# Retention and a mixture of adapters in one kernel: batch scores alternating with the next unit's transposes, the last two units interleaved, adapter weights loaded later

## The chip, the cores and the metric

The kernel runs on one core of a Trainium2 chip. The metric is the device time in microseconds, here the median of three runs. Engines are named as the profile names them: PE is TensorE (PEld its weight loads), DVE is VectorE, ACT is ScalarE, POOL is GpSimd, SP is SyncE, which issues most of the transfers.

## What is computed

Two layers, one behind the other. The first is retention: causal scores with a decay per head and without a softmax. The second is a mixture of eight low-rank adapters, two of them chosen per token.

```python
# q, k, v: (8, 8, 576, 64) fp32 = (batch, heads, sequence, head size)
scores = (q @ k.T) / sqrt(64)
gamma  = 1 - 2 ** (-5 - h)                          # one per head
ret    = (scores * gamma ** (i - j) for i >= j, else 0) @ v
x      = ret as (batch * seq, heads * head size)     # (4608, 512)
logits = x @ w_gate                                  # 8 experts
w      = softmax over the two largest logits
out    = x + sum over the two of w_e * (x @ A[e]) @ B[e]   # rank 16
```

The kernel cuts the sequence of 576 into four full chunks of 128 and a half chunk of 64. In a chunk the scores are made directly; what came before the chunk enters through a 64x64 state per head (`P`), which is updated from chunk to chunk. A quad is four batches of one chunk (that is what one set of loads brings); a unit is two batches of a quad with all eight heads. There are 16 units of full chunks (0 to 15), and two units of half chunks (16 and 17), each with four batches.

## The kernel before

Each unit goes through stages with one letter each. The order of instructions on PE, DVE and ACT is the order in which they are written; a dependency fixes it. PSUM has eight tiles of one bank (`pp`), which every stage takes from; the framework assigns them and places the waits.

```python
def mm(*args, **kw):                       # line 81: every PE instruction
    chain("pe", nc.tensor.matmul(*args, **kw))
def vec(fn, **kw):                         # line 84: DVE, but for two memsets
    chain("dve", getattr(nc.vector, fn)(**kw))
def act(fn, **kw):                         # line 87: ACT
    chain("act", getattr(nc.scalar, fn)(**kw))
...
# scale_v(t): GpSimd multiplies v of unit t by the decay, in place, 2 instructions
# stage_T(t): 16 transposes of q, two PSUM tiles (pqT), copies by ACT; then the same for k (pkT)
# stage_Q(t): query times state P into px (two tiles)          [not in the first chunk]
def stage_S(t):                            # scores of a full unit
    for b in range(2):
        ps = [pp.tile([128, HP, C], FP32, tag="pb", name=f"ps{ho}") for ho in range(2)]
        for hp in range(HP):
            for ho in range(2):
                mm(ps[ho][:, hp, :], lhsT=s["kT"][rows(ho), b, hp, :],
                   rhs=s["qT"][rows(ho), b, hp, :], start=(hp == 0), stop=True, ...)
        for ho in range(2):
            r = wk.tile([128, HP, C], FP32, tag=f"rt{ho}", name=f"rt{ho}", bufs=4)
            vec("tensor_tensor", out=r, in0=ps[ho],
                in1=tri..., op=ALU.mult)       # causal mask, out of PSUM
# half unit: scores of both halves in pe (two tiles), evicted with a mask into rh
# stage_U(t): k times v into pu; DVE adds P (pn), GpSimd scales it into the new P
# stage_R(t): scores times v, onto px; DVE multiplies by the decay of the row into xT
# stage_B(t): 16 transposes of xT into po (two tiles): the x of "x + sum"
# stage_Z(t): xT times the adapters' A and the gate (AW), into pz; then on DVE:
#             lg (logits), m8 (largest eight), ns (minus the sum of the two largest)
def stage_W(t):                            # routing weights
    for g in range(2):
        act("activation", out=sg[:, g, :], in_=lg[:, g, :], func=AFT.Sigmoid,
            bias=ns[:, g : g + 1], scale=2.0)
    for g in range(2):
        vec("scalar_tensor_tensor", out=cm[:, g, :], in0=lg[:, g, :],
            scalar=m8[:, g, 1:2], in1=sg[:, g, :], op0=ALU.is_ge, op1=ALU.mult)
    for g in range(2):                     # zc = weight * (x @ A), fp16
        vec("tensor_tensor", out=zc..., in0=pz..., in1=cm..., op=ALU.mult)
# stage_X(t): 2 transposes of zc (pzt), copied by ACT into zT
# stage_Y(t): zT times B onto po; 4 copies by ACT into osb; stores by SyncE
...
scale_v(0)
for t in range(NU):
    if units[t][2] == 0:
        issue(quads.index(units[t][:2]) + 2)     # loads, two quads ahead
    if t + 1 < NU:
        scale_v(t + 1)
    if t == 0:
        spin(12)                                 # keeps PE busy while loads come
        stage_T(0, pause=12)
        stage_T(1)
        stage_S(0)
        stage_S(1)
        for u in range(2):
            stage_Q(u); stage_U(u); stage_R(u)
        for ho in range(2):                      # AW[1] is AW[0], halves swapped
            gp.tensor_copy(out=AW[1][rows(ho)], in_=AW[0][rows(1 - ho)])
        for u in range(2):
            stage_Z(u)
        stage_T(2)
        continue
    if t == 1:
        continue
    done = [0, 1] if t == 2 else [t - 1] if t > 2 else []
    if not is_full(t):
        stage_Q(t)
    stage_S(t)
    for u in done: stage_W(u)
    if t + 1 < NU: stage_T(t + 1)
    for u in done: stage_B(u)
    if is_full(t):
        stage_Q(t)
    stage_U(t)
    stage_R(t)
    for u in done: stage_X(u)
    stage_Z(t)
    for u in done: stage_Y(u)
stage_W(NU - 1); stage_B(NU - 1); stage_X(NU - 1); stage_Y(NU - 1)
```

Loads: q, k and v of a quad are 1 MB each, in runs of 256 bytes. The first quad's are followed by the adapter weights (`load_moe`: four transfers of A in runs of 64 bytes, one of the gate, and B from GpSimd's queue), and these by the second quad's.

Of the kernel before, what the change touches and what calls it, by code (L numbers as in the profile page):

```python
# [10 lines left out]
FP32 = mybir.dt.float32  # L11
# [7 lines left out]
def kernel(  # L19
# [141 lines left out]


    nat = {}

    def issue(n):
        if n >= len(quads):
            return
        c, qd = quads[n]
        first = n == 0
        tl = [  # L170
            iop.tile([128, QUAD, H, Dh], FP32, tag=tag, name=tag) for tag in ("q32", "k32", "v32")
        ]
        if c == NFULL:
            for src, dst in zip((q, k, v), tl):
                for g in range(2):
                    nc.sync.dma_start(
                        out=dst[64 * g : 64 * g + 64, 0:2].rearrange("p s h d -> p (s h) d"),
                        in_=src[
                            QUAD * qd + 2 * g : QUAD * qd + 2 * g + 2, :, C * c : C * c + L, :
                        ].rearrange("s h j d -> j (s h) d"),  # L180
                    )
        def load(n, lo, hi):
            nc.sync.dma_start(  # L183
                out=tl[n][:, lo:hi].rearrange("p b h d -> p (b h) d"),
                in_=(q, k, v)[n][
                    QUAD * qd + lo : QUAD * qd + hi, :, C * c : C * c + C, :
                ].rearrange("b h j d -> j (b h) d"),
            )

        if first:  # L190
            for n in range(3):
                load(n, 0, 4)
                if n == 1:
                    nc.sync.dma_start(out=pack, in_=dr_pack.ap())  # L194
            load_moe()
        elif c < NFULL:
            for n in range(3):
                load(n, 0, 4)
        for sl in range(2):
            nat[(c, qd, sl)] = [x[:, 2 * sl : 2 * sl + 2] for x in tl]  # L200

# [19 lines left out]
                op=ALU.mult,  # L221
            )

    def stage_T(t, pause=0):

        q32, k32, v32 = nat[units[t]]
        s = st.setdefault(t, {})
        for src, nm in ((q32, "qT"), (k32, "kT")):
            if nm == "kT":
                spin(pause)  # L230
            dst = s[nm] = wk.tile([128, 2, HP, C], FP32, tag=nm, name=nm)
            ps = [pp.tile([128, HP, 2, L], FP32, tag="pb", name=f"p{nm}") for _ in range(2)]
            for hp in range(HP):
# [20 lines left out]
    def stage_Q(t):  # L254
        c, qd, sl = units[t]
        s = st[t]
        s["px"] = px = [
            pp.tile([128, HP, C], FP32, tag="pb", name=f"px{x}") for x in range(2)
        ]
        if c == 0:  # L260
            return
        full = is_full(t)
        for hp in range(HP):
            for y in range(1 if full else 2):
                for ho in range(2):
                    for x in range(2):
                        Pt = P[2 * qd + sl][:, :, x] if full else P[2 * qd + x][:, :, y]
                        i = slice(0, C) if full else rows(y)
                        mm(
                            px[x][rows(ho ^ x), hp, i],  # L270
                            lhsT=Pt[rows(ho), hp, :],
                            rhs=s["qT"][rows(ho), x, hp, i],
                            start=(hp == 0 and y == 0),
                            stop=False,
                            skip_group_check=True,
                        )

    def stage_S(t):
        s = st[t]
        rt = s.setdefault("rt", {})  # L280
        if not is_full(t):
# [20 lines left out]
                )  # L302
                rt[ho] = r
            return
        for b in range(2):
            ps = [pp.tile([128, HP, C], FP32, tag="pb", name=f"ps{ho}") for ho in range(2)]
            for hp in range(HP):
                for ho in range(2):
# [102 lines left out]
                    )  # L411
        s["po"] = po

    def stage_X(t):
        s = st[t]
        pzt = pp.tile([128, 2, 128], FP16, tag="pb", name="pzt")
        for g in range(2):
            mm(
                pzt[:, g, :], lhsT=s["zc"][:, g, :], rhs=ident16,
                is_transpose=True, start=True, stop=True,  # L420
            )
        zt = mo.tile([128, 2, 128], FP16, tag="zT", name="zT")
        act("copy", out=zt, in_=pzt)
        s["zT"] = zt

    def stage_Z(t):
        s = st[t]
        pz = pp.tile([128, 2, ER + E], FP32, tag="pb", name="pz")
        for g in range(2):
            for dt in range(HP):  # L430
                mm(
                    pz[:, g, :],
                    lhsT=s["xT"][g][:, dt, :],
                    rhs=AW[g][:, dt, :],
                    start=(dt == 0),
                    stop=(dt == HP - 1),
                    skip_group_check=True,
                )
        m8 = mo.tile([128, 2, E], FP32, tag="m8", name="m8")
        ns = mo.tile([128, 2], FP32, tag="ns", name="ns")  # L440
        sg = mo.tile([128, 2, E], FP32, tag="sg", name="sg")
        cm = mo.tile([128, 2, E], FP32, tag="cm", name="cm")
        lg = mo.tile([128, 2, E], FP32, tag="lg", name="lg")
        vec("tensor_copy", out=lg, in_=pz[:, :, ER : ER + E])
        for g in range(2):
            vec("max", out=m8[:, g, :], in_=lg[:, g, :])
        vec("scalar_tensor_tensor", 
            out=ns, in0=m8[:, :, 0], scalar=-1.0, in1=m8[:, :, 1],
            op0=ALU.mult, op1=ALU.subtract,
        )  # L450
        s["route"] = lg, m8, ns, sg, cm, pz

    def stage_W(t):
        s = st[t]
        lg, m8, ns, sg, cm, pz = s.pop("route")
        for g in range(2):
            act("activation", 
                out=sg[:, g, :], in_=lg[:, g, :], func=AFT.Sigmoid,
                bias=ns[:, g : g + 1], scale=2.0,
            )  # L460
        for g in range(2):
            vec("scalar_tensor_tensor", 
                out=cm[:, g, :], in0=lg[:, g, :], scalar=m8[:, g, 1:2], in1=sg[:, g, :],
                op0=ALU.is_ge, op1=ALU.mult,
            )
        zc = mo.tile([128, 2, ER], FP16, tag="zc", name="zc")
        for g in range(2):
            vec("tensor_tensor", 
                out=zc[:, g, :].rearrange("p (e r) -> p e r", e=E),
                in0=pz[:, g, 0:ER].rearrange("p (e r) -> p e r", e=E),  # L470
                in1=cm[:, g, :].unsqueeze(2).broadcast_to((128, E, R)),
                op=ALU.mult,
            )
        s["zc"] = zc

    def stage_Y(t):
        c, qd, sl = units[t]
        s = st.pop(t)
        po = s["po"]
        osb = outp.tile([128, 2, HP, 2, Dh], FP32, tag="osb", name="osb")  # L480
        bv = Bcat.rearrange("p (a o d) -> p a o d", a=HP, o=2)
        for cc in range(2):
            for g in range(2):
                mm(
                    po[cc][:, g, :, :],
                    lhsT=s["zT"][:, g, :],
                    rhs=bv[:, :, cc ^ g, :],
                    start=False,
                    stop=True,
                    skip_group_check=True,  # L490
                )
        for cc in range(2):
            for g in range(2):
                act("copy", out=osb[:, g, :, cc ^ g, :], in_=po[cc][:, g])
        of = osb.rearrange("p g a o d -> p g (a o d)")
        for g in range(2):
            for x in range(1 if c < NFULL else 2):
                bt = 2 * sl + g if c < NFULL else 2 * g + x
                n0 = S * (QUAD * qd + bt) + C * c
                if c < NFULL:  # L500
                    nc.sync.dma_start(out=out[n0 : n0 + C, :], in_=of[:, g, :])
                else:
                    nc.sync.dma_start(out=out[n0 : n0 + L, :], in_=of[rows(x), g, :])

    issue(0)
    issue(1)
# [14 lines left out]
    for t in range(NU):  # L521
# [3 lines left out]
            scale_v(t + 1)  # L525
        if t == 0:
            spin(12)
            stage_T(0, pause=12)
            stage_T(1)
            stage_S(0)  # L530
            stage_S(1)
            for u in range(2):
# [2 lines left out]
                stage_R(u)  # L535
            for ho in range(2):
                gp.tensor_copy(out=AW[1][rows(ho)], in_=AW[0][rows(1 - ho)])
            for u in range(2):
                stage_Z(u)
            stage_T(2)  # L540
            continue
        if t == 1:
            continue
        done = [0, 1] if t == 2 else [t - 1] if t > 2 else []
        if not is_full(t):
            stage_Q(t)
        stage_S(t)
        for u in done:
            stage_W(u)
        if t + 1 < NU:  # L550
            stage_T(t + 1)
        for u in done:
            stage_B(u)
        if is_full(t):
            stage_Q(t)
        stage_U(t)
        stage_R(t)
        for u in done:
            stage_X(u)
        stage_Z(t)  # L560
        for u in done:
            stage_Y(u)
    stage_W(NU - 1)
    stage_B(NU - 1)
    stage_X(NU - 1)
    stage_Y(NU - 1)
    return

# [28 lines left out]
```

## Time and profile before

| | |
|---|---|
| time, median of three runs | 206.25 us (205.06 to 207.9) |
| the profiled execution | 203.81 us, span of its instructions 202.1 us |
| PE busy | 184.5 us, 91% of the span |
| DVE, ACT, POOL busy | 109.4, 71.5, 58.3 us |
| loads and stores | 28.91 MB read, 9.44 MB written, 190 GB/s over the span |
| TensorE clock granted | 0.99 |

A unit's step is the stretch from its first score matmul to the next unit's. The table shows where some begin, read from the timeline of PE (us from the start of the span).

| event on PE | starts at |
|---|---|
| first transposes of unit 0 | 7.17 |
| scores of unit 0 | 13.12 |
| scores of unit 2 | 29.82 |
| scores of unit 3 | 42.40 |
| scores of unit 4 | 51.62 |
| scores of two later neighbours | 102.62 and 112.83 |
| stage Q of unit 16, the first half unit | 175.23 |
| stage Q of unit 17, the second | 183.97 |
| last product (`po` of unit 17) | 195.33 |

How to read the lines further down: in the page's first part each engine has its busy time, its share of the span and its count of instructions. In the chain, each line has a start, a length and what the time went to. In the timeline, a line has start, length, engine, operation, the tiles written and read, shapes and a count where neighbours were merged; the bracket at its end is the idle time of the engine before it, and what ended that. A tile keeps its name in the code without its number. Each fp32 matmul shows as two instructions, so a full unit's 16 score matmuls are 32. The profile models the ends of matmuls, so that a PE with gaps of a tenth of a microsecond or two can still show as busy.

### The profile page before, as it was taken

The numbers are of one execution on the slowest core, as the hardware profiler recorded it, in microseconds if no ns is written. First come the engines' busy times: TensorE is split into PE (matmuls) and PEld (weight loads), VectorE is DVE, ScalarE is ACT, GpSimd is POOL, SyncE is SP. The second block draws the span as 40 slices with busy tenths as digits, with TensorE's granted clock in tenths as the row PEclk, the third lists the DMA queues.
The fourth block names the chain that finished last, engine by engine and source line by source line (L and its number), as shares of the span: only waits on it lengthen the run. The fifth ranks groups of instructions, "written<-read, shape, count | busy, mean of one in ns | idle before, by whom it ended". The sixth has DMA issues, their size and how long they took to land.

```text
span 202.1 us, 8056 instructions
## 1 busy us (share of the span) xinstructions
PE 184.5 (91%) x3588; PEld 164.6 (81%) x3588; DVE 109.4 (54%) x270; ACT 71.5 (35%) x196; POOL 58.3 (29%) x68
## 2 busy tenths in 40 slices
PE   7889977999999999999999999899999999989740
PEld 2378966899999999999999999799999999978620
DVE  0249628648647565757555655646464646363420
ACT  2040054163525252525243434234343434343060
POOL 5059108043046203636203722610502060200000
PEclk9999999999999999999999999999999999999995
DMA  4996999999999949952989798439145702022044
GB/s 122 312 241 90 296 275 246 284 276 254 322 310 270 289 175 272 274 181 109 250 245 303 247 257 267 111 88 255 51 135 122 194 11 100 3 107 99 11 104 104
DMA packets 47698, 38.73 MB, mean 192 GB/s; under 512 B 18352, under 2 KB 43056, under 8 KB 47664
## 3 DMA queue, kind: packets, MB, share of 16 engines
q1 hardware_dynamic: 47520, 38.09, 66.0%
q8 instruction: 28, 0.46, 1.0%
q0 software_dynamic: 144, 0.13, 0.4%
q14 instruction: 6, 0.05, 0.1%
HBM read 28.91 MB, written 9.44 MB: 190 GB/s over the span
## 4 chain that ended last, share of the span: by engine, by line
PE 79%; DVE 7%; SPq 4%; DMA 3%; ACT 2%; POOL 1%; issue 1%; ACTq 0%; POOLq 0%
PE px L81 22%; PE pz L81 17%; PE ps L81 13%; PE po L81 9%; PE pu L81 9%; PE pkT L81 3%; PE pqT L81 3%; DMA v<-in_v_dram 3%; DVE rt L84 2%; SPq L183 2%; DVE cm L84 2%; SPq L194 2%; PE pzt L81 2%; POOL v L217 1%; ACT osb L87 1%
## 5 line engine op out<-in xcount | busy, mean ns | idle before, releaser
L84 DVE TENSOR_TENSOR rt<-ps,tri 128x512 f32<-128x512 f32 x64 | 39.6, 682 | 13.4 <-PE ps L81 13.4
L217 POOL TENSOR_TENSOR v<-v,pack 128x512 f32<-128x512 f32 x36 | 36.5, 1043 | 23.7 <-DMA v<-in_v_dram 23.7
L349 POOL TENSOR_TENSOR P<-pn,gdec 128x512 f32<-128x512 f32 x12 | 15.3, 1273 | 82.2 <-DVE pn L84 82.2
L81 PE MATMUL pz<-AW,xT 128*128 128x136 f32 x288 | 37.2, 283 | 1.1 <-DVE xT L84 1.1
L81 PEld LDWEIGHTS pz<-AW,xT 128*128 128x128 f32 x288 | 34.5, 190 | 1.6 <-DVE xT L84 1.6
L81 PE MATMUL ps<-qT,kT 64*128 64x128 f32 x512 | 32.6, 278 | 1.6 <-ACT kT L87 1.4
L81 PEld LDWEIGHTS ps<-qT,kT 64*128 64x128 f32 x512 | 29.7, 188 | 4.6 <-PE po L81 2.7
L87 ACT COPY osb<-po 128x256 f32<-128x256 f32 x72 | 21.5, 389 | 30.0 <-PE po L81 28.2
L81 PE MATMUL px<-rt,v 128*64 128x128 f32 x512 | 30.8, 273 | 0.0
L84 DVE TENSOR_TENSOR xT<-px,asc 128x512 f32<-128x512 f32 x36 | 24.7, 691 | 7.3 <-PE px L81 6.0
L87 ACT COPY qT<-pqT 128x512 f32<-128x512 f32 x32 | 17.2, 590 | 31.3 <-PE pqT L81 31.3
L81 PEld LDWEIGHTS px<-rt,v 128*64 128x64 f32 x512 | 27.8, 137 | 0.0
L87 ACT COPY zT<-pzt 128x256 f16<-128x256 f16 x18 | 6.6, 373 | 53.8 <-PE pzt L81 53.8
L87 ACT COPY kT<-pkT 128x512 f32<-128x512 f32 x36 | 19.6, 608 | 9.7 <-PE pkT L81 9.7
L81 PE MATMUL pu<-v,k 128*64 128x64 f32 x512 | 18.6, 225 | 1.4 <-DVE zc L84 1.0
L81 PEld LDWEIGHTS pu<-v,k 128*64 128x64 f32 x512 | 16.4, 138 | 3.9 <-issue 3.1
L84 DVE TENSOR_TENSOR pn<-pu,P 128x512 f32<-128x512 f32 x12 | 8.3, 691 | 20.4 <-PE pu L81 20.4
L81 PE MATMUL po<-id,xT 64*128 64x64 f32 x288 | 15.7, 229 | 2.2 <-DVE zc L84 1.6
L84 DVE COPY lg<-pz 128x16 f32<-128x16 f32 x18 | 3.1, 174 | 25.8 <-PE pz L81 25.8
L81 PEld LDWEIGHTS po<-id,xT 64*128 64x128 f32 x288 | 12.1, 139 | 4.4 <-DVE rt L84 2.4
L81 PE MATMUL px<-qT,P 64*64 64x128 f32 (+1 forms) x512 | 15.6, 262 | 0.0
L81 PEld LDWEIGHTS px<-qT,P 64*64 64x64 f32 x512 | 12.5, 133 | 1.3 <-issue 0.4
(42 smaller groups left out, 147.3 us busy)
## 6 DMA issues: line engine op xcount, KB each, us to landing
out_dram<-osb SPq DMA_DIRECT2D x32, 256.0 KB, 3.3
q<-in_q_dram SPq DMA_DIRECT2D x4, 256.0 KB, 4.4
k<-in_k_dram SPq DMA_DIRECT2D x4, 256.0 KB, 3.7
v<-in_v_dram SPq DMA_DIRECT2D x4, 256.0 KB, 4.0
out_dram<-osb SPq DMA_DIRECT2D x8, 128.0 KB, 2.3
AW<-in_moe_A_dram SPq DMA_DIRECT2D x4, 64.0 KB, 3.5
q<-in_q_dram SPq DMA_DIRECT2D x8, 0.2 KB, 6.3
k<-in_k_dram SPq DMA_DIRECT2D x8, 0.2 KB, 9.1
```

The costliest lines, as they stand in the source:

```text
L81: chain("pe", nc.tensor.matmul(*args, **kw))
L84: chain("dve", getattr(nc.vector, fn)(**kw))
L87: chain("act", getattr(nc.scalar, fn)(**kw))
L183: nc.sync.dma_start(out=tl[n][:, lo:hi].rearrange("p b h d -> p (b h) d"), in_=(q, k, v)[n][QUAD * qd + lo : QUAD * qd + hi, :, C * c : C ...
L194: nc.sync.dma_start(out=pack, in_=dr_pack.ap())
L217: nc.gpsimd.tensor_tensor(out=vv[:, b], in0=vv[:, b], in1=gv[:, 0 if is_full(t) else 1].unsqueeze(2).broadcast_to((128, H, Dh)), op=ALU.mult,)
L349: nc.gpsimd.tensor_tensor(out=Pt, in0=pn, in1=gdec, op=ALU.mult)
```

## The change

1. **Scores and transposes alternate.** In a full unit's step, the scores of the first batch come first, then the q transposes of the next unit, then the scores of the second batch, then the k transposes. The sigmoid (new stage V) is issued on ACT ahead of the q copies. This is to give DVE time to empty the first two score tiles while PE does something else.
2. **The start.** The q transposes of units 0 and 1 come before the k transposes of both. Unit 0's routing and output are done before unit 2 begins, with the transposes of unit 2 between Z(0) and Z(1). Before, units 0 and 1 were both routed in step 2.
3. **The adapter weights** are loaded behind the second quad's q instead of ahead of it.
4. **The last two units** (half chunks) are interleaved; the final one is handled in two halves, so that the routing of one lies beside matmuls of the other, and its output copies are split between ACT and DVE. To have it so, unit 16 holds batches 0, 1, 4 and 5, and unit 17 the others; their loads are one set of six transfers for all eight batches.

```diff
@@ load of quads @@
         if c == NFULL:
+            if qd > 0:
+                return
             for src, dst in zip((q, k, v), tl):
                 for g in range(2):
-                    nc.sync.dma_start(... 2 batches of the quad, 64 rows ...)
+                    nc.sync.dma_start(... 4 batches of one half of the batches, 64 rows ...)
...
-            load_moe()
-        elif c < NFULL:
+        else:
             for n in range(3):
                 load(n, 0, 4)
+                if quads[1] == (c, qd) and n == 0:
+                    load_moe()
@@ stage_T, stage_S: in parts @@
-    def stage_T(t, pause=0):
+    def stage_T(t, names=("qT", "kT")):
...
-    def stage_S(t):
+    def stage_S(t, bs=(0, 1)):
...
-        for b in range(2):
+        for b in bs:
@@ X, Z, W, Y take gs, the halves they work on; V is cut out of W @@
+    def stage_V(t, gs=BOTH):           # the sigmoids
...
+    def stage_Y(t, gs=BOTH, spread=False):
...
+                if spread and cc == 1:
+                    vec("tensor_copy", out=osb[:, g, :, cc ^ g, :], in_=po[cc][:, g])
+                else:
+                    act("copy", out=osb[:, g, :, cc ^ g, :], in_=po[cc][:, g])
@@ the loop @@
             spin(12)
-            stage_T(0, pause=12)
-            stage_T(1)
+            stage_T(0, ("qT",))
+            stage_T(1, ("qT",))
+            spin(10)
+            stage_T(0, ("kT",))
+            stage_T(1, ("kT",))
             stage_S(0)
             stage_S(1)
...
-            for u in range(2):
-                stage_Z(u)
-            stage_T(2)
+            stage_Z(0)
+            stage_W(0)
+            stage_T(2, ("qT",))
+            stage_Z(1)
+            stage_T(2, ("kT",))
+            stage_B(0)
+            stage_X(0)
+            stage_Y(0)
             continue
...
+        if t == NU - 1:
+            break
+        if is_full(t):
+            stage_S(t, (0,))
+            stage_V(t - 1)
+            stage_T(t + 1, ("qT",))
+            stage_S(t, (1,))
+            stage_W(t - 1)
+            stage_T(t + 1, ("kT",))
+            stage_B(t - 1)
             stage_Q(t)
+            stage_U(t)
+            stage_R(t)
+            stage_X(t - 1)
+            stage_Z(t)
+            stage_Y(t - 1)
+            continue
+
+        stage_Q(t)                      # t = 16
         stage_S(t)
+        stage_W(t - 1)
+        stage_T(t + 1)
+        stage_B(t - 1)
         stage_R(t)
+        stage_Q(t + 1)
+        stage_X(t - 1)
         stage_Z(t)
+        stage_W(t)
+        stage_Y(t - 1)
+        stage_S(t + 1)
+        stage_B(t)
+        stage_X(t)
+        stage_R(t + 1)
+        stage_Y(t)
+        for g in range(2):
+            stage_Z(t + 1, (g,))
+            stage_W(t + 1, (g,))
+        stage_B(t + 1)
+        for g in range(2):
+            stage_X(t + 1, (g,))
+            stage_Y(t + 1, (g,), spread=True)
```

## The prediction

> **What bounds the kernel now.** I read the page first, for engine shares and the chain that ended last.
>
> ```profile
> span 202.1 us, 8056 instructions
> ...
> PE 184.5 (91%) x3588; PEld 164.6 (81%) x3588; DVE 109.4 (54%) x270; ACT 71.5 (35%) x196; POOL 58.3 (29%) x68
> ...
> PE 79%; DVE 7%; SPq 4%; DMA 3%; ACT 2%; POOL 1%; issue 1%; ACTq 0%; POOLq 0%
> ```
>
> TensorE is the bound: 79% of the chain. The change takes away no arithmetic (same matmuls, transposes and evictions), so it can only close holes in TensorE's stream. The view by stretches tells where they are (columns: length, then busy time of PE, weight load, DVE, ACT, POOL, clock, DMA share, GB/s).
>
> ```profile
> 0.00:27.00 27.00, 23.88 (x314) 17.82 (x314) 12.29 (x24) 3.60 (x6) 10.86 (x24) 1.00 0.85 214
> 27.00:42.40 15.40, 12.08 (x221) 10.94 (x221) 8.65 (x23) 6.06 (x17) 4.05 (x4) 1.00 0.96 272
> 42.40:123.00 80.60, 80.44 (x1553) 74.30 (x1552) 49.37 (x119) 32.72 (x92) 28.98 (x27) 1.00 0.85 253
> 123.00:134.30 11.30, 10.30 (x201) 9.44 (x200) 7.21 (x17) 4.06 (x12) 5.32 (x5) 1.00 0.53 141
> 134.30:175.20 40.90, 40.78 (x793) 37.55 (x792) 23.15 (x62) 15.98 (x45) 9.11 (x8) 1.00 0.41 112
> 175.20:202.10 26.90, 17.01 (x515) 14.55 (x514) 8.76 (x31) 9.03 (x29) 0.00 (x0) 0.92 0.28 80
> ```
>
> The holes are in unit 2's step (3.3 us idle of 15.4), one step near 123 us (1.0 of 11.3) and the tail of the two half chunks (9.9 of 26.9). The thirteen full steps between (units 3 to 15) look full. I then read the chain in order of time (start, length, what) for the first hole:
>
> ```profile
> 27.72 0.67 ACT qT L87 x2
> 28.39 0.28 issue
> 28.67 1.10 ACT kT L87 x2
> 29.82 1.21 PE ps L81 x16
> 31.03 2.46 DVE rt L84 x4
> 33.49 1.87 DVE cm L84 x2
> 35.36 0.41 DVE zc L84 x2
> 35.82 0.71 PE po L81 x15
> ```
>
> Unit 2's scores wait for its own transposes' copies; then two routings queue behind the four score evictions, and a transpose waits for `zc`. That `cm`, 1.87 us here, is usually 0.35 for two. The timeline of VectorE and GpSimd around the other hole shows the cause:
>
> ```profile
> 125.27 4.05 POOL L217 TENSOR_TENSOR v<-v,pack 128x512 f32<-128x512 f32 x4 [4.33 <-DMA v<-in_v_dram]
> ...
> 126.62 1.72 DVE L84 SCALAR_TENSOR_TENSOR cm<-lg,m,sg 128x8 f32<-128x8 f32 x2
> ...
> 128.88 1.15 PE L81 MATMUL pu<-v,k 128*64 128x64 f32 x32 [0.98 <-DVE zc L84]
> ```
>
> The pair ends at 128.34, just as the third of GpSimd's 1.01 us `v` scalings does (125.27 + 3 x 1.01 = 128.30). Last, inside a "full" step, the weight loads:
>
> ```profile
> 104.40 0.63 PEld L81 LDWEIGHTS pqT<-id,q 64*128 64x128 f32 x16
> 104.95 0.59 PEld L81 LDWEIGHTS pkT<-id,k 64*128 64x128 f32 x16
> 105.45 0.14 PEld L81 LDWEIGHTS po<-id,xT 64*128 64x128 f32 x1
> 105.75 0.57 PEld L81 LDWEIGHTS po<-id,xT 64*128 64x128 f32 x15 [0.16 <-DVE rt L84]
> 106.39 0.86 PEld L81 LDWEIGHTS px<-qT,P 64*64 64x64 f32 x32
> ```
>
> `po` begins at 105.45, takes one transpose and stops until 105.75: it wants a PSUM bank that a score eviction still reads. `po` undisturbed takes 0.64 us in the tail (178.72 to 179.36); here it takes 0.94. So about 0.28 us per step is lost that the busy share hides.
>
> [...] `cm` reads `lg` and `sg`, both in SBUF; the longest took 1.077 us against a median of 0.218. [...] 80.44 busy of 80.60 conceals the 0.28 above. [...] the trace shows the score evictions (0.62 apart) falling behind the scores (0.95 us for two).
>
> **The change, part by part.**
>
> Start. The four transposes of units 0 and 1 are regrouped, but the scores still wait for k and then for ScalarE's copies (13.12), and R(1) still ends near 23.0, paced by `v` (15.57) and GpSimd. No gain there. The adapter loads go behind quad 1's q. Quad loads land about 4.05 us apart (v at 31.3 and 43.3 are three loads apart), so the adapter weights land near 23.3 instead of before 19.6, and their swapped copy (GpSimd, 1.3) near 24.7. Z(0) then runs 23.3 to 24.3, waits, 24.8 to 25.8: a loss of about 0.9. In return W(0)'s VectorE/ScalarE chain lies beside T(2) of q, Z(1), T(2) of k (0.5 + 1.9 + 0.5, to 28.7) and B(0); X(0) waits for the copies of kT ahead of zT on ScalarE (1.1), Y(0) ends near 31.0. S(2) starts then, no longer followed by unit 0's B, X, Y (1.4) or held by two routings. Step 2 takes about 9 instead of 12.6 (29.82 to 42.40), so S(3) starts near 40.0: gain 2.4. But `v` of quad 2 lands at 43.3 as before, DMA being at 0.96; in the earlier step 3 its scaling now meets `cm`, and Z(3) waits some 0.6 to 0.8. Start: **1.7**.
>
> Steady steps. Before, the second bank that `po` takes is that of the third score tile, free at 105.68. With two score tiles, two transposes, two score tiles, two transposes, eight banks being reused in the order they come free, I expect `po` to get the banks of the first two, free by 105.1: the 0.28 goes. Against it two more changes between matmuls and transposes, each 0.05 (scores to transposes, 104.46 to 104.51) to 0.14 (16 transposes take 0.50 before more transposes, 0.64 before matmuls). Net about 0.1 x 13: **1.3**.
>
> Collisions of `cm` with GpSimd. W still follows all four evictions, so the exposure stays; where they fall depends on when `v` lands. I allow **0.3** of the 1.0 us.
>
> Tail, from the start of Q(16), with lengths from the tail before: Q16 to 0.9, S16 2.0, T17 3.1, B15 3.75, R16 5.0, Q17 6.0, X15 6.1, Z16 8.0 (its `xT` was made under Q17; before, it waited 0.73), Y15 8.6, S17 9.65, B16 10.3, X16 10.6. R17 waits for the second `rh` (behind W16's routing on VectorE, 11.7), 12.9; Y16 13.4; Z17 waits for xT, 13.8 to 15.75; B17 16.4 covers the first half's routing; X, zT, Y of half 0 to 17.5, of half 1 to 18.75; two copies in parallel on ScalarE and VectorE 19.35. Two stores instead of four, 0.6 each: 20.6; and the 2.96 us from the last issue (199.14) to the end: 23.6 instead of 26.9. **3.3**.
>
> The half chunk's loads become 6 instead of 12; they have been waited for by nothing on the chain: 0.
>
> Sum: 1.7 + 1.3 + 0.3 + 3.3 = 6.6, and 206.25 − 6.6 = 199.6. The tail is conservatively counted, so I round to 199.3.
>
> **The rivals.** (1) The alternation makes a new PSUM wait: the second score pair then needs a bank of `po` of the unit before, which ScalarE empties in 1.20 us beginning at 102.51. I reckon that free at 103.1 for a tile wanted at 104.1, but the assignment isn't visible. A stall of 0.3 per step would cost 4 us and leave about 204. (2) The later adapter weights cost more than reckoned: they are 64-byte runs, DMA moves only 21 to 106 GB/s between 15.2 and 19.2, and SyncE took 6.37 us to issue them. Sitting in front of k1 they can hold T(2), k1 being due near 27.5. The start would then bring nothing: 201. (3) Nothing in the steady step: 201. (4) The optimistic one: the whole 0.28, no collisions, 2.4 at the start, 4 in the tail: 195.
>
> **Range and chances.** Tail gain is nearly certain (2.5 to 4), start 0 to 3, steps −2 to 3. Together 195.5 to 203. Two per cent is 202.1; missing it needs rival 1, or 2 and 3 together. Faster 0.83, same 0.15, slower 0.02.
>
> **What would show it.** The tail from Q(16) to the end about 23.6; S(3) starting near 40; a step near 10.1 with `po` taking 0.64 between its first weight load and Q's; Z(0) waiting for AW. Wrong, if score matmuls show idle behind `osb` or `rt`, or if `cm` of over 1 us turns up in more steps than three.

## The result and the profile after

| | before | after |
|---|---|---|
| time, median of four runs each | 205.66 us (204.39 to 207.9) | 195.03 us (194.63 to 195.82) |
| ratio, 95% interval | | 0.951 (0.944 to 0.957) |
| span of the profiled execution | 202.1 us | 193.2 us |

The head of the page of the changed kernel:

```profile
span 193.2 us, 8031 instructions
...
PE 180.5 (93%) x3586; PEld 162.5 (84%) x3586; DVE 109.7 (57%) x274; ACT 72.7 (38%) x195; POOL 58.3 (30%) x68
```

The work is the same. PE's count and the other engines' busy times have hardly moved, and only the holes are fewer. PE's busy time fell by 4.0 us, although it does the same matmuls: part of what was closed had been counted as busy.

The view by stretches of the changed kernel, cut where units begin (start to Z(0), to S(2), S(3), S(4), Q(16), end):

```profile
0.00:23.36 23.36, 18.72 (x278) 13.65 (x278) 11.44 (x20) 3.57 (x6) 9.55 (x22) 1.00 0.81 203
23.36:31.44 8.08, 6.96 (x87) 5.98 (x87) 2.25 (x13) 2.91 (x8) 1.32 (x3) 1.00 0.97 278
31.44:40.36 8.92, 8.92 (x168) 8.43 (x167) 5.62 (x14) 4.10 (x12) 3.99 (x4) 1.00 0.92 266
40.36:49.74 9.38, 9.13 (x167) 8.47 (x166) 6.66 (x17) 4.10 (x12) 4.05 (x4) 1.00 0.81 244
49.74:169.72 119.98, 119.77 (x2377) 111.58 (x2377) 73.50 (x182) 49.28 (x133) 39.38 (x36) 1.00 0.72 208
169.72:193.20 23.48, 16.98 (x515) 14.39 (x514) 10.19 (x35) 8.77 (x28) 0.00 (x0) 0.91 0.32 92
```

Unit 2's step is full now (8.92 busy of 8.92). Set beside the same cuts of before, the 8.9 us between the two spans split so:

| stretch | before | after | gain | predicted |
|---|---|---|---|---|
| start of the span to S(4) | 51.62 | 49.74 | 1.88 | 1.7 |
| S(4) to Q(16), twelve steps | 123.61 | 119.98 | 3.63 | 1.3 + 0.3 |
| Q(16) to the end | 26.87 | 23.48 | 3.39 | 3.3 |

Of the first line, 0.52 belongs to the first k, which landed at 10.73 instead of 11.25. What is left, 1.36, is the order of work. The middle line was predicted at less than half its size.

A step before had its `po` stop. The weight loads of the changed kernel in the step that starts at 100.05 (start, length, tiles written and read, count):

```profile
100.93 0.63 PEld L81 LDWEIGHTS pqT<-id,q 64*128 64x128 f32 x16
101.47 0.98 PEld L81 LDWEIGHTS ps<-qT,kT 64*128 64x128 f32 x16
102.37 0.63 PEld L81 LDWEIGHTS pkT<-id,k 64*128 64x128 f32 x16
102.92 0.58 PEld L81 LDWEIGHTS po<-id,xT 64*128 64x128 f32 x16
103.57 0.86 PEld L81 LDWEIGHTS px<-qT,P 64*64 64x64 f32 x32
```

`po` is one line of 16 now, with no wait in it: 102.92 to 103.57 is 0.65 us, where it was 0.94. Eleven of the twelve steps take 9.95 to 9.96; before, the undisturbed ones took 10.19 to 10.26.

The collision, from the timeline of the changed kernel over all engines:

```profile
123.21 4.04 POOL L226 TENSOR_TENSOR v<-v,pack 128x512 f32<-128x512 f32 x4 [5.34 <-DMA v<-in_v_dram]
123.80 1.48 DVE L84 SCALAR_TENSOR_TENSOR cm<-lg,m,sg 128x8 f32<-128x8 f32 x2
124.51 1.15 PE L81 MATMUL pu<-v,k 128*64 128x64 f32 x32
125.20 0.48 DVE L84 TENSOR_TENSOR zc<-pz,cm 128x128 f16<-128x128 f32 x2
```

It is still there: `cm` takes 1.48 under a `v` scaling. But `pu` begins 0.69 before `zc`, so it no longer waits for it. This step, 119.95 to 129.91, took 9.96, like its neighbours; before, such a step took 11.25.

Then the start, where Z(0) and Y(0) wait (PE's timeline):

```profile
23.39 1.17 PE L81 MATMUL pz<-AW,xT 128*128 128x136 f32 x8 [0.49 <-issue]
24.86 1.19 PE L81 MATMUL pz<-AW,xT 128*128 128x136 f32 x8 [0.31 <-POOL AW L570]
...
30.90 0.61 PE L81 MATMUL po<-Bcat,zT 128*128 128x256 f16 x4 [0.79 <-ACT zT L87]
31.44 1.16 PE L81 MATMUL ps<-qT,kT 64*128 64x128 f32 x16
```

And the tail of the changed kernel:

```profile
176.12 2.07 PE L81 MATMUL pz<-AW,xT 128*128 128x136 f32 x16
...
183.23 2.12 PE L81 MATMUL pz<-AW,xT 128*128 128x136 f32 x16 [0.23 <-DVE xT L84]
...
186.96 0.39 PE L81 MATMUL po<-Bcat,zT 128*128 128x256 f16 x2 [0.73 <-ACT zT L87]
...
187.98 0.39 PE L81 MATMUL po<-Bcat,zT 128*128 128x256 f16 x2 [0.36 <-ACT zT L87]
...
188.41 0.42 DVE L84 COPY osb<-po 128x256 f32<-128x256 f32 x1 [0.54 <-PE po L81]
```

Z(16) follows without a wait; before, PE stood idle for 0.56 ahead of it, for `xT`. The last product starts at 187.98, 18.26 after Q(16); before it was 20.10 after (195.33 − 175.23), and its copies then ran for 1.20 more on ScalarE alone. The other 1.55 us of the gain lie behind that product: copies on two engines, and two stores instead of four after the last.

### The profile page after: what moved, and what is told of

Read it like the earlier page. It is cut to its first block, busy times and chain, and to the rows that moved or that the text cites. A ratio compares the mean times of both kernels' runs of the same rounds, so it can differ in the third digit from the quotient of the medians.

```text
span 193.2 us, 8031 instructions
## 1 busy us (share of the span) xinstructions
PE 180.5 (93%) x3586; PEld 162.5 (84%) x3586; DVE 109.7 (57%) x274; ACT 72.7 (38%) x195; POOL 58.3 (30%) x68
## 5 line engine op out<-in xcount | busy, mean ns | idle before, releaser
L84 DVE TENSOR_TENSOR rt<-ps,tri 128x512 f32<-128x512 f32 x64 | 41.0, 686 | 18.7 <-PE ps L81 14.4
L81 PE MATMUL pz<-AW,xT 128*128 128x136 f32 x288 | 37.7, 283 | 1.3 <-issue 0.5
L81 PE MATMUL ps<-qT,kT 64*128 64x128 f32 x512 | 35.7, 281 | 0.7 <-ACT kT L87 0.7
L81 PEld LDWEIGHTS ps<-qT,kT 64*128 64x128 f32 x512 | 31.0, 188 | 3.7 <-PE po L81 2.7
L87 ACT COPY zT<-pzt 128x256 f16<-128x256 f16 (+1 forms) x19 | 6.9, 361 | 48.9 <-PE pzt L81 48.9
L84 DVE COPY lg<-pz 128x16 f32<-128x16 f32 (+1 forms) x19 | 3.3, 173 | 25.8 <-PE pz L81 25.8
L87 ACT ACTIVATE sg<-lg,ns 128x8 f32<-128x8 f32 x36 | 9.4, 318 | 17.6 <-DVE ns L84 17.6
L81 PE MATMUL pqT<-id,q 64*128 64x64 f32 x288 | 11.9, 223 | 1.4 <-DMA q<-in_q_dram 1.4
```

## Experiments

All are variants of the changed kernel with parts put back, or of the kernel before. The half units keep their new grouping of batches and their six loads in every variant of the changed kernel. Each was timed in three rounds or more beside the kernel before on the same chip; a ratio is to those runs. The three parts of the change each gain less than 2% alone, so their intervals are wide beside their gains, and the stretches of the traces tell more.

### One part at a time

**alt_only**: the alternation alone; the start, the place of the adapter weights and the tail as before.

```diff
-            stage_Z(0); stage_W(0); stage_T(2, ("qT",)); stage_Z(1)
-            stage_T(2, ("kT",)); stage_B(0); stage_X(0); stage_Y(0)
+            stage_Z(0); stage_Z(1); stage_T(2)
 ...                                   # adapter weights ahead of the second quad, units 16 and 17 in turn
```

> Only the alternation of scores and transposes (units 2 to 15), with the old start, the old tail and the adapter weights ahead of quad 1. Bank theory (the steady gain is that po no longer waits for the third score eviction and pu no longer for zc): a full step of 9.95 us instead of 10.20, no 1 us loss where cm meets a v scaling, first score of unit 4 to Q of unit 16 in 119.5 to 120.5 us instead of 123.6; in all 3 to 5 us faster than before. Rival (the step got shorter because the new start shifted when v lands, so that collisions fell elsewhere): the step stays at 10.1 to 10.2 and the gain is under 2 us.

Measured: 202.5 us, ratio 0.987 (0.979 to 0.995). S(4) to Q(16) took 119.94, as in the changed kernel, and Q(16) to the end 27.06, as before. So the whole gain of the steps comes from the alternation. One step of the twelve took 10.45, and its lines say why (VectorE, GpSimd, weight loads):

```profile
61.56 2.04 POOL L225 TENSOR_TENSOR v<-v,pack 128x512 f32<-128x512 f32 x2
...
61.91 0.71 DVE L84 SCALAR_TENSOR_TENSOR ns<-m 128x2 f32<-128x2 f32 x1
...
63.69 0.85 PEld L81 LDWEIGHTS ps<-qT,kT 64*128 64x128 f32 x13 [0.20 <-DVE rt L84]
```

Here the `v` scaling met `ns`, normally 0.16, which stands ahead of the score evictions; the second pair of score tiles then lacked a bank. A hold ahead of the evictions still costs. By its ratio the run gained 2.7 us, less than the 3 to 5 expected, while the stretch came out as expected.

**start_only**: the new start and the later adapter weights alone.

```diff
-            stage_S(t, (0,)); stage_V(t - 1); stage_T(t + 1, ("qT",))
-            stage_S(t, (1,)); stage_W(t - 1); stage_T(t + 1, ("kT",))
+            stage_S(t); stage_V(t - 1); stage_W(t - 1); stage_T(t + 1)
 ...                                   # units 16 and 17 in turn
```

> Only the new start (with the adapter weights behind quad 1's q), steps and tail as before. Expected from the two traces: unit 3's scores at 40 to 41 us instead of 42.4, step 10.20, 1 to 3 us faster in all. If the parts are not additive (the start's gain eaten by a later wait for v), under 1 us.

Measured: 202.98 us, ratio 0.988 (0.980 to 0.996). In the profiled execution the first k landed late, at 12.68, so its instants are read from there: S(4) 39.39 us after it, against 40.37 before and 39.01 with the whole change. The steps are 10.20 again, but for one of 11.55 (123.48 to 135.03), where a pair of `cm` was held for 2.02 and `pu` waited 1.28 for `zc`, as it did before.

**tail_only**: the interleaved tail alone.

```diff
 ...                                   # start, adapter weights and full steps as before
         stage_Q(t)                    # t = 16
         stage_S(t)
         stage_W(t - 1); stage_T(t + 1); stage_B(t - 1); stage_R(t)
         stage_Q(t + 1); stage_X(t - 1); stage_Z(t) ...
```

> Only the interleaved last two units. Expected: Q of unit 16 to the end 23.3 to 23.8 us instead of 26.9, 3 to 4 us faster in all. If the tail's gain needed the alternation's bank order, under 2.5 us.

Measured: 202.26 us, ratio 0.986 (0.979 to 0.993). Q(16) to the end took 23.44, against 23.48 with the whole change; the steps 10.20 with one of 11.08. By the ratios the three parts bring 1.3%, 1.2% and 1.4%, each give or take 0.8. Their sum, 3.9%, agrees with the 4.9% of the whole within that. The parts add up as far as these runs can tell, and none visibly gives back what another wins. The tail's time gained 2.9 us by its ratio, where 3 to 4 was expected.

**tail_whole**: the changed kernel, with the last unit's Z, W, X and Y whole instead of by halves.

```diff
-        for g in range(2):
-            stage_Z(t + 1, (g,)); stage_W(t + 1, (g,))
+        stage_Z(t + 1); stage_W(t + 1)
         stage_B(t + 1)
-        for g in range(2):
-            stage_X(t + 1, (g,)); stage_Y(t + 1, (g,), spread=True)
+        stage_X(t + 1); stage_Y(t + 1)
```

> The changed kernel with the interleaved tail, but the last unit routed and written out whole, as before, instead of in two halves with copies on two engines. From the traces: the halves overlap 1.0 to 1.3 us of routing and save about 0.6 us of copies and stores at the end; 0.8 to 2 us slower than the changed kernel. If interleaving the two units is all of the tail's gain: within 0.4 us.

Measured: 197.27 us, ratio 0.959 (0.953 to 0.965); Q(16) to the end 25.53. PE's timeline shows the waits that the halves had covered:

```profile
187.08 0.43 PE L81 MATMUL pzt<-ident,zc 128*128 128x128 f16 x2 [1.14 <-DVE zc L84]
188.03 0.61 PE L81 MATMUL po<-Bcat,zT 128*128 128x256 f16 x4 [0.52 <-ACT zT L87]
```

So of the 3.39 us of the tail 2.05 (25.53 − 23.48) are the halves with the split copies, and 1.34 the interleaving of units 16 and 17.

### The start: adapter weights and loads

**moe_first**: the changed kernel with the adapter weights ahead of the second quad, as before.

```diff
+            load_moe()                # behind the first quad
 ...
-                if quads[1] == (c, qd) and n == 0:
-                    load_moe()
```

> The changed kernel, but with the adapter weights ahead of quad 1 again. By the prediction's reckoning Z of unit 0 then starts at 22.9 to 23.1 instead of 23.39 and its second half does not wait for the swapped copy; but quad 1's q lands near 23.2 and k where it did, so unit 2's k transposes stay bound by the same landing (27.3 to 27.6). Expected: the same within 0.7 us, or up to 0.9 faster. If the placement is what makes the new start work, 1 us slower or more.

Measured: 196.08 us, ratio 0.956 (0.950 to 0.962). S(3) starts 29.4 after the first k's landing, against 29.63 with the weights later. The place of the weights alone is worth nothing that these runs can tell: the median is 1.05 us above the changed kernel's, but the intervals of the two ratios overlap. The instants are a rough comparison, since in this execution the scores of units 0 and 1 took 5.47 us (from 14.17) where the changed kernel's took 3.84, as they would with about 3.3 us at half the clock (an estimate from the two lengths), and the second quad's k was transposed at 29.83, against 28.69.

**split_head**: an attempt at a better start. The first quad's loads are halved, the adapter weights follow at once, units 0 and 1 are finished before unit 2, and GpSimd scales `v` ahead of its other work.

```diff
-            for n in range(3):
-                load(n, 0, 4)
+            for lo in (0, 2):
+                for n in range(3):
+                    load(n, lo, lo + 2)
+            load_moe()
```

> The changed kernel with a start that goes after what is left there: TensorE begins its scores at 12.6 us, because it waits for whole-quad loads. The first quad's loads are cut into halves of two batches, unit by unit, the adapter weights follow directly, GpSimd scales v of unit 0 ahead of its constants, and units 0 and 1 are run one after the other and both finished before unit 2. Expected: scores of unit 0 at 8 to 10 us, of unit 3 at 37 to 39 instead of 40.4; 1.5 to 4 us faster than the changed kernel. If the landing of quad 1's k and v (27 and 31 us) sets the start whatever the first quad does: under 1 us.

Measured: 196.75 us, ratio 0.960 (0.952 to 0.968): no better. Unit 0's scores start at 9.86 instead of 12.60, but S(2) at 32.80 instead of 31.44 and S(3) at 40.76 instead of 40.36. The 1.5 to 4 us expected did not come. PE's timeline says what held unit 2:

```profile
30.14 0.61 PE L81 MATMUL po<-Bcat,zT 128*128 128x256 f16 x4 [1.14 <-ACT zT L87]
30.68 0.71 PE L81 MATMUL pkT<-id,k 64*128 64x64 f32 x16
32.80 1.16 PE L81 MATMUL ps<-qT,kT 64*128 64x128 f32 x16 [1.41 <-ACT kT L87]
...
35.82 1.15 PE L81 MATMUL pu<-v,k 128*64 128x64 f32 x32
```

The second quad's k was issued at 19.20 and landed near 28.3, an estimate from the median of 9.1 that loads of k took in the profile of before. Its transposes stand behind unit 1's output in this order, which waited for ScalarE, and began at 30.68; the scores then waited for ScalarE again. `v` landed near 32.5 (its scaling, which waited for it, began at 32.59), and `pu`, the first to use it, began at 35.82 without a wait. So it was this order, with ScalarE's copies in it, and not the loads, that held unit 2. Whether an order with k's transposes ahead of unit 1's output would gain was not tried. The changed kernel keeps the lowest median of all that ran.

### What the alternation removes, and what it costs

**q_between**: old start and tail, no alternation. Only stage Q moves between the q and the k transposes, so `po` comes 1.0 us later and its bank is long free.

```diff
             stage_S(t)
             stage_W(t - 1)
-            stage_T(t + 1); stage_B(t - 1); stage_Q(t)
+            stage_T(t + 1, ("qT",)); stage_Q(t); stage_T(t + 1, ("kT",)); stage_B(t - 1)
             stage_U(t)
```

> The earlier run with U ahead of B also moved the state's update ahead of Q, so it could not answer. Here, with scores not alternating and the old start and tail, only Q moves: between the q and the k transposes of the next unit, so that po asks for its banks 1.03 us later and the banks it gets are those of the fourth score tile and the first q tile. Bank theory: the 0.3 us stop inside po goes; against it two changes of tile shape more (0.11 us each), so a step of 9.95 to 10.1 instead of 10.20 and 1 to 3.5 us faster than before. Rival (alternating scores with transposes is itself what shortens the step): the step stays at 10.2 to 10.4, time same or slower.

Measured: 203.95 us, ratio 0.988 (0.979 to 0.997). S(4) to Q(16), all of it at a granted clock of 1.00, took 121.65 against 123.61; a step 10.05. The weight loads of one:

```profile
107.65 0.86 PEld L81 LDWEIGHTS px<-qT,P 64*64 64x64 f32 x32
108.69 0.58 PEld L81 LDWEIGHTS pkT<-id,k 64*128 64x128 f32 x16 [0.17 <-issue]
109.18 0.58 PEld L81 LDWEIGHTS po<-id,xT 64*128 64x128 f32 x16
109.83 1.01 PEld L81 LDWEIGHTS pu<-v,k 128*64 128x64 f32 x32
```

`po` takes 0.65 (109.18 to 109.83) without a stop. So the bank was what stopped it (which bank the trace doesn't show), and time alone, without alternation, cures it. It gains 0.15 per step where the alternation gains 0.25: the q transposes, now ahead of Q's 64x64 tiles, take 0.59 (107.07 to 107.66) where they took 0.50. One step, 125.27 to 136.31, still cost about 1 us for `cm`.

**fine_alt**: the changed kernel with scores and transposes alternating twice as often, by groups of 8: four changes more per step.

```diff
+            for b, nm in ((0, "qT"), (1, "kT")):
+                for h2 in ((0, 1), (2, 3)):
+                    stage_S(t, (b,), h2)
+                    stage_T(t + 1, (nm,), h2)      # V and W where they were
```

> The changed kernel with scores and transposes alternating twice as finely: four more changes between matmuls and transposes in each of 14 steps, nothing else. As predicted (0.05 to 0.14 us for a change): 3 to 6 us slower than the changed kernel. If a change between the two costs nothing because both use tiles of 64 rows by 128 columns: within 1 us of the changed kernel, step 9.9 to 10.05.

Measured: 201.33 us, ratio 0.983 (0.975 to 0.991), 6.3 us over the changed kernel, of which the twelve steps are 4.1 (124.08 against 119.98): one takes 10.33, which is 0.38 more than 9.95. Most of that isn't the changes themselves (weight loads):

```profile
106.23 0.54 PEld L81 LDWEIGHTS ps<-qT,kT 64*128 64x128 f32 x8
106.68 0.14 PEld L81 LDWEIGHTS pkT<-id,k 64*128 64x128 f32 x1
106.99 0.26 PEld L81 LDWEIGHTS pkT<-id,k 64*128 64x128 f32 x6 [0.17 <-DVE rt L84]
```

The four groups of scores take 2.04 together against 1.94 in two groups: 0.1 for the four changes, 0.03 each. A further 0.2 is a new stop: with each pair of score tiles spread over a longer stretch, its evictions begin later and `pkT` lacks a bank. The rest lies in `po` (0.65 instead of 0.60) and Q (1.08 instead of 1.04), for a reason that doesn't show. So the 3 to 6 us expected came nearly true for the wrong reason: a change costs 0.03, not 0.05 to 0.14, and a bank that comes late costs more.

**u_first**: old order, with U and then B ahead of Q.

```diff
             stage_T(t + 1)
+            stage_U(t)
             stage_B(t - 1)
             stage_Q(t)
-            stage_U(t)
             stage_R(t)
```

> Scores not alternating, old start and tail; in a full step the product U (one PSUM tile) is moved ahead of the transposes B, so that po asks for its banks about 0.95 us later. Bank theory: po takes 0.60 to 0.66 us again instead of 0.94 and the step falls to 9.9 to 10.0 without any alternation; 2.5 to 4 us faster than before. Rival (alternating itself, by lying loads of weights beside matmuls of another kind, makes the step shorter): the step stays at 10.15 or more.

Measured: 225.12 us, ratio 1.095 (1.086 to 1.104). The time says nothing about the banks. With U first, Q multiplies by the state after its update instead of the state that the reference uses, and so waits in each step for DVE's `pn` and GpSimd's scaling of P (1.56 us at 95.83). What can be read is `po` ahead of that wait: in the step from 89.50, its 16 weight loads run from 93.56 to 94.13 without a stop, as the bank theory said.

### Does a hold of `cm` cost?

Two runs with the same extra load: from unit 4 on, GpSimd multiplies a score tile from SBUF by the mask, twice per unit, released by the third score eviction. Its product isn't used. In each step it meets `cm`.

```diff
             vec("tensor_tensor", out=r, in0=ps[ho], in1=tri..., op=ALU.mult)
+            if b == 1 and ho == 0 and t >= 4:
+                for _ in range(2):
+                    gp.tensor_tensor(out=junk, in0=r, in1=tri..., op=ALU.mult)
```

**junk_before** has it in the old order:

> Old order in all parts, and in each full unit from 4 on two additional GpSimd instructions (1.04 us each, reading SBUF, result unused), released when the third score tile is evicted, so that they meet cm in every step. Bank theory: cm is held, zc comes 1.2 to 1.5 us later, pu waits for zc's bank: 8 to 14 us slower than before. If a held cm costs TensorE nothing in general and the 1 us at 128 us had another cause: under 3 us.

**junk_after** in the changed kernel:

> The changed kernel with the same additional GpSimd instructions in units 4 to 15. Bank theory: cm is held as long as in the old order, but pu does not wait for zc; only the eviction of px into xT is late by a little: 0 to 4 us slower than the changed kernel. Rival (the alternating order is as sensitive): 8 us slower or more.

Measured: junk_before 211.14 us, ratio 1.031 (1.023 to 1.039); S(4) to Q(16) 128.56, which is 4.95 more than the kernel before. junk_after 196.05 us, ratio 0.958 (0.951 to 0.965); the same stretch 119.49, against 119.98 without the load. `cm` is held alike in both: its 36 instructions take 19.0 us in junk_before (10.4 in the kernel before) and 18.5 in junk_after (8.8 in the changed kernel). One step of junk_before:

```profile
131.92 2.62 POOL L333 TENSOR_TENSOR junk<-rt,tri 128x512 f32<-128x512 f32 x2 [5.32 <-DVE rt L84]
...
132.29 1.07 DVE L84 SCALAR_TENSOR_TENSOR cm<-lg,m,sg 128x8 f32<-128x8 f32 x2
...
133.28 0.48 DVE L84 TENSOR_TENSOR zc<-pz,cm 128x128 f16<-128x128 f32 x2
...
133.90 1.15 PE L81 MATMUL pu<-v,k 128*64 128x64 f32 x32 [0.33 <-DVE zc L84]
```

and one of junk_after:

```profile
113.54 2.63 POOL L334 TENSOR_TENSOR junk<-rt,tri 128x512 f32<-128x512 f32 x2 [1.18 <-DVE rt L84]
...
113.91 1.06 DVE L84 SCALAR_TENSOR_TENSOR cm<-lg,m,sg 128x8 f32<-128x8 f32 x2
...
114.55 1.15 PE L81 MATMUL pu<-v,k 128*64 128x64 f32 x32
...
114.90 0.47 DVE L84 TENSOR_TENSOR zc<-pz,cm 128x128 f16<-128x128 f32 x2
```

In the old order `pu` follows `zc`, in the new one it begins before it. The hold is the same, and only in the old order does it reach PE. There ten of the twelve steps take 10.49 to 10.61, 0.3 to 0.4 more than 10.20, with `pu` right behind `zc`: 3.7 us together. The other two take 11.42, because `pu` waited for the `v` scaling that the extra load had delayed (1.15 us at 102.13, 1.10 at 166.49). The effect has the expected sign but not the expected size of 8 to 14 us: a pair of `cm` was held for 0.7, not 1.2 to 1.5.

### The clock at the start

The profile of q_between showed something else ahead of S(4), by stretches (the third figure from the end is the granted clock):

```profile
26.00:29.00 3.00, 3.00 (x38) 2.81 (x36) 1.03 (x8) 0.00 (x0) 0.00 (x0) 1.00 0.90 276
29.00:32.20 3.20, 0.88 (x22) 0.69 (x18) 0.12 (x1) 2.28 (x6) 0.00 (x0) 0.98 0.89 243
32.20:35.50 3.30, 3.30 (x32) 3.30 (x34) 1.27 (x2) 0.63 (x4) 1.56 (x2) 0.51 1.00 280
```

After 3.2 us in which PE was mostly idle (for k, then for the copies of kT) its clock fell to half, from 32.05 to 35.46, and unit 2's scores took 3.63 us instead of 2.06. junk_before shows the same from 36.81 to 40.23. The profile of the kernel before has the same holes (1.45 and 1.55 us) and no dip (its clock is 1.00 from 27 to 43); in moe_first, with the new start, the long scores of units 0 and 1 look like one. The mean clock of the single runs seemed to say that the dip is common in the kernel before: it was under 0.982 in 12 of 21 of its runs by then, and in 1 of 24 of the six kernels with the new start (split_head, with its own start, had 1 of 4). So I tried to fill the first hole.

**warm_before**: the kernel before, with five dummy matmuls into the score tile of unit 2, ahead of its scores, which overwrite them.

```diff
             ps = [pp.tile(...) for ho in range(2)]
+            if t == 2 and b == 0:
+                for _ in range(5):
+                    mm(ps[0]..., lhsT=idle[:, 0:128], rhs=idle, start=True, stop=True)
```

> The kernel before, with five dummy matmuls (0.23 us each, 1.15 us in all) in the idle stretch ahead of unit 2's scores (idle 1.45 us in the profile of before); their product is overwritten, nothing is left out. Two profiles of kernels with the old start showed the TensorE clock at half speed for about 3.4 us right after this stretch or the next one; of 21 runs of the kernel before 12 had a mean clock under 0.982, of 24 runs of kernels with the new start 1 had. If idle time at the start is what lowers the clock, fewer of these runs should lie under 0.982 (one or two of six) and the median should be 0.5 to 1.5 us below the kernel before on the same chip, with the step of unit 2 no longer than before in the trace. If only the loads' landing spreads the times, the clocks and the median stay as before (ratio 0.998 to 1.002). If the second idle stretch (the transpose that waits for zc, 1.55 us) is what does it, the clocks stay low too: then the runs do not tell the two holes from the rival.

Measured: 205.9 us (15 runs), ratio 1.004 (1.001 to 1.008). The clock was under 0.982 in 8 of 15 runs, in 12 of 20 of the kernel before beside it. Filling this hole, in the profile from 1.45 to 0.45 us, changes nothing for the better. The hole at `zc` (1.26 in this kernel's profile) remained, so this doesn't tell whether idle time is the cause.

The profiles also show that the mean clock was a poor witness. warm_before's profiled execution has a mean of 0.982 without any dip at the start: its clock was 1.00 up to 170 and 0.89 from there to the end at 202.0, where that of the kernel before was 0.94 from 170 on (it stood at half from 197.97 to the end at 202.1). And moe_first's has 0.984 with the long scores at its start. So the counts above mix the start with the end, and how often the start is hit isn't known.

What PE did in the 3.41 us ahead of the two falls can be read: in q_between (28.64 to 32.05) it was busy for 1.16 us, in junk_before (33.40 to 36.81) for 2.21, and in both with nothing but transposes. Whether the transposes have to do with the fall was not tested.

## Why the prediction was right, and where not

The direction was right and so was the main idea, that only holes in PE's stream can be won. The size was too small: about 7 us were forecast, and the medians show 10.6. The median of 195.03 lies 0.5 below the low end of the range in microseconds. The kernel before also ran faster beside it than the 206.25 that the prediction started from: the ratio times 206.25 gives 196.1, inside the range. That range is not the sum of its parts either: gains of 0.5 to 10 us give 196.3 to 205.8, where 195.5 to 203 was written.

**The start (1.7; measured 1.88, or 1.36 without the luck of the first k).** Z(0) at 23.39 and its second half at 24.86 behind AW's copy were predicted at 23.3 and 24.8; S(3) at 40.36, predicted near 40.0. S(2) came 0.4 later than reckoned, and Z(3)'s idle wait for `xT` was 0.25, less than the 0.6 to 0.8 said. The second rival, adapter weights that cost more than reckoned, didn't show: moe_first is the same within what its runs can tell.

**The steady steps (1.3; measured 0.25 a step).** The `po` stop went as predicted, all 0.28 of it; q_between confirms that a bank was behind it. What failed is the term set against it, "two more changes between matmuls and transposes, each 0.05 [...] to 0.14". Measured, the two together cost about 0.03: within a step, S, T and S, T take 0.99 + 0.49 + 0.95 + 0.49 = 2.92 where S and T took 1.89 + 0.50 + 0.50 = 2.89. The 0.14 was misread: 16 transposes do take 0.11 longer ahead of a tile of another shape (0.60 ahead of Q's 64x64, 0.49 ahead of `ps` or `po`, from start to start on PE), but scores and transposes both load tiles of 64x128. The step held such a switch once before and holds it once now. Twelve steps times 0.245 make 2.9 us, and three steps of before had been longer by 0.05.

**Collisions (0.3; measured about 1.0).** The failed step is what was drawn from "W still follows all four evictions, so the exposure stays", namely that the cost stays too. `cm` is still held: two pairs over 1 us in the changed kernel, at 44.20 and 123.80. What went is the dependent. Before, `pu` got the bank that `zc` empties; now it begins while `cm` still runs (124.51, with `cm` until 125.28), and the next thing on PE to need `zc` is `pzt`, 2.8 us later (124.51 to 127.34). junk_after holds `cm` in every step for nothing; junk_before pays. Without any extra load the same collision cost 0.7 to 1.4 in one step of each other profile with the old order (start_only, tail_only, q_between, warm_before), while alt_only held a pair for 1.18 at 125.81 in a step of 9.96. Against the 1.05 us of the vanished collision stands a stop in one step of the changed kernel, 10.49 instead of 9.95. The profile gives it to "issue" at 75.79, after three of R's 32 instructions. moe_first has it at the same instruction of the same unit (77.39, a step of 10.49), so it isn't the chance of one execution; its cause stays open. Together: 2.9 + 0.16 + 1.05 − 0.54 = 3.6, the middle line of the table.

**The tail (3.3; measured 3.39).** The sketch from Q(16) gave 23.6, measured 23.48. Z(16) without a wait and the halves covering each other's routing are as said; the wait before was 0.56 of idle time in PE's timeline, not 0.73.

**The rivals.** No new PSUM wait at `osb` came in the steps (the first rival). The fourth had the right parts for the steps, the whole 0.28 and no collisions; its 195 also held 2.4 for the start and 4 for the tail, which didn't come, so that its number fits the median is luck.

**What stays open.** The profiles differ by 8.9 us; the medians by 10.6, or by 9.7 to 10.4 against the kernel before on the other chips (204.7 to 205.4). The profile of before was among its quickest runs. The first k's transposes, which wait for its landing, begin at 10.6 to 13.0 in the profiles of kernels with the same first loads, and a dip of the clock can cost up to about 1.7 us, an estimate from the 3.41 us at half speed in q_between (unit 2's scores took 1.57 longer there). How the rest divides between these wasn't settled.

## What to carry to other kernels

When several stages take from one pool of PSUM banks, the order in which they take them decides who waits for whom (here `po` took 0.94 us in one order and 0.65 in the other): ask of each tile whose eviction frees its bank. Alternating two kinds of work with the same weight tile shape was nearly free here (0.03 us a change) and gave evictions time to run beside matmuls. A held instruction costs through whoever waits for it: here the same hold of `cm` made ten of the twelve steps 0.3 to 0.4 us longer in the old order and none in the new one (119.49 against 119.98 for the twelve). So look for its dependent before paying for the hold.

## What the runs showed of the hardware

- `cm`, a VectorE instruction that reads `lg` and `sg` from SBUF, took longer under GpSimd's instructions: a pair took 1.06 us instead of 0.36 under two of 1.3 us each (junk_after). `ns`, with its small operands from SBUF, took 0.71 instead of 0.16 under a `v` scaling (alt_only).
- The clock fell to half for 3.41 us in q_between (32.05 to 35.46) and for 3.42 in junk_before (36.81 to 40.23). In the 3.41 ahead of that PE was busy for 1.16 us and for 2.21, with transposes. What brings a dip, and why the same holes bring one in one execution and not in another, no run here shows.
- A change between fp32 scores and fp32 transposes, both of 64x128 weights, costs 0.03 us (fine_alt, 0.10 for four); 16 transposes ahead of a differently shaped weight tile take 0.60 instead of 0.49 (the changed kernel).
